# z1 of the last token chunk by seven block products, with the input weights scaled to fp16 in place

## The chip, the cores and the metric

The kernel runs on one core of one Trainium2 chip. The metric is the device time of one execution in microseconds (us); lower is better. The engines of the core are TensorE (PE, with its weight loads shown as PEld), VectorE (DVE), ScalarE (ACT), GpSimd (POOL) and SyncE (SP, which only issues DMAs here).

## The reference

One transformer-like block on 2048 tokens of 1024 channels, in bf16. First a local attention (8 keys at distance 2), then a gated MLP whose gate mixes over tokens:

```python
h  = x + A(layernorm(x))          # attention: qkv product, windowed softmax, output product
def B(x):                          # x = layernorm(h), 2048 x 1024
    z  = gelu(x @ w_in)            # w_in is 1024 x 3584
    z1 = z[:, :1792]
    z2 = layernorm(z[:, 1792:])
    g  = w_sp @ z2 + b_sp          # w_sp is 2048 x 2048: the spatial product
    return (z1 * g) @ w_out        # w_out is 1792 x 1024
out = h + B(layernorm(h))
```

## The kernel before

The 2048 tokens are worked in four chunks of 512 (CH). Up to the gate, all work is recorded as operations with a cost, a priority and dependencies in an object `Order`; its `run()` plans them with these costs on a model of the engines and the buffers and then emits them in the planned order, which is fixed from then on. Each engine works its instructions off in that order. What the plan says of times has no effect on the chip; waits come from the data and from reused memory.

The stages, in the order of time: q, k and v products; attention of the chunks 0 to 3 on DVE, under PE's products; `head(c)` (output product L719, residual `res` L725, layer norm, transposition of the normalized tokens into hnT by DMA on SP's queue); `b_z2(c)` (L796: z2 with the tokens as weights of the array, gelu and square on ACT, normalization on DVE, stores); `b_z1(c)` (L864: z1 transposed, features on the partitions; the input weights are the array's weights, 512 tokens the moving operand). Each chunk has seven pairs of 128-feature tiles; a pair fills one accumulator of two PSUM banks (`acc`, three of them), 16 matmuls of 512 columns, and ACT's gelu (L870) writes it out as z1s, whose row sums go to `zsum` and which a DMA stores in z1_d. The input weights of z1 lie in win2 (four pairs) and win3 (three pairs), bf16.

Then comes the spatial stage, written out by hand. It multiplies in blocks: a 2x2 partition of both factors is multiplied with seven products instead of eight (the Strassen and Winograd scheme), with sums and differences of blocks as operands, called forms. `load_raw` brings w_sp transposed into rawa and rawb, `scale_raw` (L958) scales it to fp16 by powers of two, `t_forms` (L965 to L971) makes three forms of it in the tiles form0 to form2 and one in place, `z_form` (L989) makes the forms of z2, which is read back from z2_d by `load_z2f`. `bias_rows` (L948) multiplies the scaled rows with the bias, from a tile `brow` in the pool bph. These are DVE operations of the planned part. Then the pools bph, ln1 and ps_acc are closed, and the pools p2 and psB open in the same memory. For each feature pair n, `row_one` multiplies the first block product into a bank `banka` (two of them) and ACT copies it to a tile p1 of p2; the products k4, k3 and k2 follow; `row_two` adds the second block product into the same `banka`:

```python
    def row_one(n, b11):
        firsts[n] = bank_a(), f32("p1", 3)
        times(firsts[n][0][:], slab(z2f[n][0][:, :, 0:P]), slab(b11), True)
        A.copy(firsts[n][1][:], firsts[n][0][:])

    def row_two(n, b21):
        times(firsts[n][0][:], slab(z2f[n][1][:, :, 0:P]), slab(b21), False)
```

DVE and POOL combine the products, multiply with z1 (read back by `load_z1c`, scaled by `z1_scaled` with the scales from `feature_scales`) and write zg, the operand of the output product, which is also done in blocks.

Of the kernel before, what the change touches and what calls it, by code (L numbers as in the profile page):

```python
# [10 lines left out]
FP32 = mybir.dt.float32  # L11
BF16 = mybir.dt.bfloat16
FP16 = mybir.dt.float16
# [9 lines left out]
P = 128  # L23
# [45 lines left out]
class Order:  # L69
# [6 lines left out]
    def add(self, eng, us, fn, deps=(), prio=5.0, lat=0.1, take=None, free=None, table=None):  # L76
        o = _Op()
        o.eng, o.us, o.fn, o.prio, o.lat, o.free, o.table = eng, us, fn, prio, lat, free, table
        o.take = (take,) if isinstance(take, str) else take or ()
        o.deps = [d if isinstance(d, tuple) else (d, d.lat) for d in deps if d is not None]  # L80
        o.start, o.end, o.n = None, None, len(self.ops)
        self.ops.append(o)
        return o
# [49 lines left out]
def kernel(  # L133
# [47 lines left out]
    rscT = cpool.tile([P, P], BF16, name="rscT")  # L181
    rinv = cpool.tile([P, NT], I32, name="rinv_w")
    zsum = mv1[:].rearrange("p a b -> p (a b)")[:, 0:NCH * (NF // 2)].rearrange("p (c f) -> p c f", c=NCH)
    babs = rstd1[:]

    w16 = ctx.enter_context(tc.tile_pool(name="w16", bufs=2))

# [9 lines left out]
    def new_acc():  # L197
        return ps_acc.tile([P, 2, CH], FP32, name="acc", tag="acc")
# [202 lines left out]
    def dma_op(us, fn, deps, lat=0.1, free=None):  # L401
        return add("DMA", us, fn, deps, lat=lat, free=free)
# [46 lines left out]
    def order():  # L449
        seq[0] += 1  # L450
        return 6.0 + seq[0] * 1e-3
# [402 lines left out]
    def b_z1(c):  # L854
        for fp in range(NF // 2):
            deps = [G["hnT", c], G["win", 2 if fp < 4 else 3]]
            for j, k0 in PIECES:
                def mm(j=j, k0=k0, fp=fp):
                    f = 2 * fp + j
                    wt, f0 = (wins[2], f) if f < 8 else (wins[3], f - 8)  # L860
                    if j == 0 and k0 == 0:
                        G["accy", c, fp] = new_acc()
                    for kt in range(k0, k0 + 4):
                        T.matmul(G["accy", c, fp][:, j, :].rearrange("p (a b) -> p a b", a=TPC), wt[:, kt, f0 * P:(f0 + 1) * P],  # L864
                                 hnTs[c][:, :, kt, :], start=(kt == 0), stop=(kt == KT - 1))
                m_ = add("PE", 0.8634, mm, deps, prio=order(), take="acc" if j == 0 and k0 == 0 else None)
                deps = [(m_, 0.0)]
            def ev(fp=fp):
                z1s = l1.tile([P, 2, CH], BF16, name="z1s", tag="xn", bufs=4)
                A.activation(z1s[:], G["accy", c, fp][:], ACTF.Gelu_apprx_tanh, accum_out=zsum[:, c, fp:fp + 1])  # L870
                last_store[:] = [(A.dma_start if c == NCH - 1 else dma)(z1_d[2 * fp:2 * fp + 2, :, c * CH:(c + 1) * CH].rearrange("f p s -> p f s"), z1s[:])]
            e_ = add("ACT", 0.93, ev, [m_], prio=2.0, free="acc", table="gelu", take="xn")
            dma_op(3.0, lambda: None, [e_], free="xn")
        G["z1done", c] = m_
        G["z1ev", c] = e_

    wsp_view = B_w_sp.rearrange("t (a p) -> t a p", p=P)
    raw, frm, wt_ = {}, {}, {}
# [2 lines left out]
    def wsp_sums():  # L881
        tl = {}
        for i in range(TPP):
            def ld(i=i):
                load_wn(i, l1, "x4k", 4)
            gate = add("DMA", WSP_FROM + WSP_EVERY * i, lambda: None)
            l_ = dma_op(8.0, ld, [gate, wabs_ops[i - 4] if i >= 4 else G["normed", 2]])
            if i >= WSP_HELD[0]:
                l_ = add("DMA", WSP_HELD[1], lambda: None)
            for hf in range(2):  # L890
                a_ = add("ACT", 1.22, lambda i=i, hf=hf: row_sum(i, hf), [l_], prio=5.8)
            wabs_ops.append(a_)
# [17 lines left out]
    def row_scales(pr):  # L910
        n = slice(pr * TPP, (pr + 1) * TPP)
        V.tensor_tensor(wlim[:, n], wabs[:, n, 0], wabs[:, n, 1], op=ALU.add)
        V.tensor_tensor(wlim[:, n], wlim[:, n], babs[:, n], op=ALU.add)
        V.tensor_scalar(wlim[:, n], wlim[:, n], 2.0 ** -40, 2.0 ** 60, op0=ALU.max, op1=ALU.min)
        V.tensor_scalar(wexp[:, n], wlim[:, n].bitcast(I32), 0x7F800000, None, op0=ALU.bitwise_and)
        V.tensor_scalar(rsc[:, n], wexp[:, n], -1.0, float(261 << 23), op0=ALU.mult, op1=ALU.add)
        V.tensor_scalar(rinv[:, n], wexp[:, n], float(-(7 << 23)), None, op0=ALU.add)
        V.tensor_copy(rsc16[:, n], rsc[:, n].bitcast(FP32))
# [33 lines left out]
            raw[c] = wtile([P, NT, CH], "rawa", "wB") if c % 2 == 0 else zpools["z"].tile([P, NT, CH], BF16, name="rawb")  # L952
        nc.sync.dma_start_transpose(raw[c][:, :, lo * P:hi * P], wsp_view[c * CH + lo * P:c * CH + hi * P])

    def scale_raw(c, k0):
        ks = slice(k0, k0 + HK)
        rows = wt_["rows"][:, c * CH:(c + 1) * CH].unsqueeze(1).to_broadcast([P, HK, CH])
        V.tensor_tensor(raw[c][:, ks, :].bitcast(FP16), raw[c][:, ks, :], rows, op=ALU.mult)  # L958

    def t_forms(pr, n):  # L960
        a, b = raw[2 * pr][:].bitcast(FP16), raw[2 * pr + 1][:].bitcast(FP16)
        if n < 3:
            frm[pr, n] = zpools["z"].tile([P, HK, CH], FP16, name=f"form{n}")
        if n == 0:
            V.tensor_tensor(frm[pr, 0][:], b[:, 0:HK, :], a[:, 0:HK, :], op=ALU.subtract)  # L965
        elif n == 1:
            V.tensor_tensor(frm[pr, 1][:], b[:, HK:NT, :], frm[pr, 0][:], op=ALU.subtract)
        elif n == 2:
            V.tensor_tensor(frm[pr, 2][:], a[:, HK:NT, :], frm[pr, 1][:], op=ALU.subtract)
        else:  # L970
            V.tensor_tensor(b[:, 0:HK, :], b[:, HK:NT, :], b[:, 0:HK, :], op=ALU.subtract)  # L971
# [42 lines left out]

    G["open"].deps.append((G["win", 1], 0.1))
    wsp_sums()
    for c in range(NCH):
        attention(c)
        if c == 2:
            G["win", 1].deps.append((G["kload", c], 0.1))  # L1020
        if c < NCH - 1:
            head(c)
# [15 lines left out]
        bias_in(0)  # L1038

    head(NCH - 1)  # L1040
    bt_ = add("PE", 0.1, bias_turned, [G["normed", 3]], prio=1.0, take="acc", lat=0.2)
    bs_ = add("ACT", 0.3, bias_size, [bt_], prio=2.0, free="acc")
    rs_ = add("DVE", 1.0, lambda: row_scales(0), [G["avdone", NCH - 1], bs_] + wabs_ops, prio=2.8)
    rt_ = add("PE", 0.1, rows_turned, [rs_], prio=0.5, take="acc", lat=0.2)
    ro_ = add("ACT", 0.3, rows_out, [rt_], prio=1.0, free="acc")
    rl_ = dma_op(4.0, rows_first, [(ro_, 2.5), G["close"]])
    b_z2(NCH - 1)
    b_z1(NCH - 1)
    r0_ = dma_op(4.0, lambda: load_raw(0, 0, 1), [G["close"], rl_.deps[0], (G["hnT", NCH - 1, 2], 0.0 - 3.9)])
    r0_ = dma_op(4.0, lambda: load_raw(0, 1, 2), [r0_, (G["hnT", NCH - 1, 3], 0.0 - 3.9)])  # L1050
    r0_ = dma_op(8.0, lambda: load_raw(0, 2, TPC), [r0_, (G["hnT", NCH - 1, 3], 0.0 - 3.9)])
    r1_ = dma_op(10.5, lambda: load_raw(1), [r0_])
    prev = []
    for c, r_ in ((0, r0_), (1, r1_)):
        for k0 in (0, HK):
            prev = [add("DVE", 2.3, lambda c=c, k0=k0: scale_raw(c, k0), [r_, rl_] + prev, prio=3.5)]
    z_ld = {}
    for n in range(2):
        for hf in range(2):
            z_ld[n, hf] = dma_op(6.0, lambda n=n, hf=hf: load_z2f(n, hf), [r1_] + [G["z2st", 2 * hf + c, il] for c in range(2) for il in range(TPC)])  # L1060
    for n in (0, 3):
        prev = [add("DVE", 2.3, lambda n=n: t_forms(0, n), prev, prio=3.6)]
    prev = [add("DVE", 0.7, lambda: z_form(0, 3), [z_ld[0, 0]] + prev, prio=3.6)]
    for n in (1, 2):
        prev = [add("DVE", 2.3, lambda n=n: t_forms(0, n), prev, prio=3.6)]
    for m in (1, 2, 4):
        prev = [add("DVE", 0.7, lambda m=m: z_form(0, m), [z_ld[0, 0], z_ld[0, 1]] + prev, prio=3.65)]
    add("DVE", 0.7, lambda: bias_rows(0), prev, prio=3.7)
    o_.run()
    wout_a = wtile([P, 8, D], "wout_a", "wA")  # L1070
# [36 lines left out]
    def row_two(n, b21):  # L1107
        times(firsts[n][0][:], slab(z2f[n][1][:, :, 0:P]), slab(b21), False)
# [18 lines left out]
    kb = p2.tile([P, 8], BF16, name="kb", tag="kb", bufs=1)  # L1127
    ones = p2.tile([1, P], BF16, name="ones", tag="ones", bufs=1)

    def pow2_of(out, x, sign, bias):  # L1130
        V.tensor_scalar(out.bitcast(I32), x.bitcast(I32), 0x7F800000, None, op0=ALU.bitwise_and)
        V.tensor_scalar(out.bitcast(I32), out.bitcast(I32), sign, float(bias << 23) if bias > 0 else -float(-bias << 23), op0=ALU.mult, op1=ALU.add)

    def feature_scales():
        V.tensor_reduce(zmax, zsum.rearrange("p c f -> p f c"), axis=AX.X, op=ALU.add)
        V.tensor_scalar(zmax, zmax, 800.0, 2.0 ** 60, op0=ALU.add, op1=ALU.min)
        pow2_of(sf, zmax, -1.0, 253)
        pow2_of(rf, zmax, 1.0, 1)

# [75 lines left out]
    for pr in range(NCH // 2):  # L1215
# [5 lines left out]
        for i in range(NQ):  # L1221
# [7 lines left out]
                zg = p2.tile([P, NF, 2 * CH], FP16, name="zg", tag="zg", bufs=1)  # L1229
            load_wout(n)  # L1230
            z1c = z1cs[n][:].bitcast(FP16)
            if n not in firsts:
                row_one(n, b11)
            k1, p1 = firsts[n]
# [14 lines left out]
            if pr == 0 and i == 5:  # L1249
# [4 lines left out]
                T.transpose(turned[0:1, P:2 * P], kb[:, 0:1], ident[:])  # L1254
                A.copy(rscT[0:TPP, :], turned[0:TPP, 0:P])
                A.dma_start(rs_d[TPP:NT, :], rscT[0:TPP, :])
            if n not in (NQ, NQ + 1):
                row_two(n, b21)
            times(k4[:], slab(a22), slab(t4_), False)
            nc.gpsimd.tensor_tensor(p7[:], p7[:], p5[:], op=ALU.add)  # L1260
# [207 lines left out]
```

## Time and profile before

| what | value |
|---|---|
| median of 3 runs | 690.81 us (690.63 to 690.89) |
| the profiled execution | 690.56 us, span 688.8 us |
| mean granted TensorE clock | 0.999 |
| PE busy | 683.4 us, 99% of the span |
| DVE busy | 563.1 us, 82% |
| ACT busy | 338.0 us, 49% |
| POOL busy | 148.1 us, 22% |
| z1, L864: 448 matmuls of 128x512 | 98.0 us of PE, a quarter of it for the last chunk |
| z2, L796: 512 matmuls | 98.0 us of PE |
| t_forms, L965 to L971, per pair of chunks | 4 operations of 2.28 to 2.29 us on DVE |

Times of the trace are counted from the span's start. The busy time of an engine is the time in which it works on an instruction; register, semaphore and DMA-issuing instructions are not in it. A matmul's own length in the trace (0.379 us for 512 columns) holds its way through the array; in a row, matmuls start closer than that.

### The profile page before, as it was taken

The page shows a single profiled execution, that of the slowest core. Times are in us where ns is not written, and L with a number is a line of the kernel's source. Part 1 is how long each engine was busy: PE and PEld are TensorE (multiplying, and loading weights), DVE is VectorE, ACT ScalarE, POOL GpSimd, SP SyncE. Part 2 cuts the span into 40 slices and gives each one's busy share as a digit, 9 for nine tenths or more (in the row PEclk, how much of TensorE's full clock was granted, in tenths as well). Part 3 has the DMA queues.
Part 4 walks back from the last instruction along what each step waited for, and adds up shares of the span by engine and source line. Part 5 has one row for each costly group of instructions (what it writes and reads, how often), then busy time and mean ns, then how long its engine had stood idle before and what let it go on. Part 6 is the DMA issues. An engine that isn't in the chain of part 4 may idle for free.

```text
span 688.8 us, 8981 instructions
## 1 busy us (share of the span) xinstructions
PE 683.4 (99%) x3374; PEld 354.2 (51%) x3374; DVE 563.1 (82%) x701; ACT 338.0 (49%) x487; POOL 148.1 (22%) x134
## 2 busy tenths in 40 slices
PE   9999999999999999999999999999999999999997
PEld 7766666566645445444544444444444444444443
DVE  6899899998999989998995358666789998665575
ACT  4547652354236886664882553387771122324121
POOL 0100010010110101100120131443441223553442
PEclk9999999999999999999999999999999999999999
DMA  9979588667995569453583999889968214552031
GB/s 326 325 242 246 176 194 268 154 164 265 227 349 212 111 246 237 154 175 98 130 217 128 209 239 323 273 242 289 250 186 215 89 62 118 157 152 94 0 119 65
DMA packets 145275, 133.05 MB, mean 193 GB/s; under 512 B 68752, under 2 KB 117296, under 8 KB 145104
## 3 DMA queue, kind: packets, MB, share of 16 engines
q1 hardware_dynamic: 132720, 88.93, 45.1%
q0 software_dynamic: 7856, 32.97, 17.0%
q10 hardware_dynamic: 4656, 10.59, 4.5%
q8 instruction: 26, 0.43, 0.3%
q14 instruction: 17, 0.14, 0.1%
HBM read 75.25 MB, written 33.10 MB: 157 GB/s over the span
## 4 chain that ended last, share of the span: by engine, by line
PE 98%; DMA 0%; DVE 0%; ACT 0%; issue 0%; DVEq 0%
PE bank L1092 25%; PE acc L464 22%; PE acc L796 14%; PE acc L864 14%; PE banka L1092 10%; PE acc L719 8%; PE acc L306 2%; PE bank L1343 1%; PE banka L1343 0%; DMA xp<-in_A_x_dram 0%; PE L L558 0%; PE pb L620 0%; PE tpt L302 0%; DVE bnst L261 0%; ACT xnT L303 0%; DVE hr L1428 0%
## 5 line engine op out<-in xcount | busy, mean ns | idle before, releaser
L864 PE MATMUL acc<-hnT,win 128*128 128x512 bf16 x448 | 98.0, 379 | 0.0
L796 PE MATMUL acc<-win,hnT 128*128 128x512 bf16 (+1 forms) x512 | 98.0, 352 | 0.0
L796 PEld LDWEIGHTS <-hnT 128*128 128x128 bf16 x512 | 49.9, 98 | 47.4 <-issue 0.7
L528 DVE TENSOR_TENSOR prod<-qT,kT 128x4096 bf16<-128x4096 bf16 x32 | 72.9, 2287 | 1.3 <-ACT kT L470 1.3
L1092 PEld LDWEIGHTS <-zs 128*128 128x128 f16 x448 | 43.7, 98 | 52.6
L864 PEld LDWEIGHTS <-win 128*128 128x128 bf16 x448 | 43.7, 98 | 52.6 <-issue 0.7
L475 ACT CAST stg<-acc 128x1024 bf16<-128x1024 f32 x36 | 36.4, 1012 | 60.7 <-PE acc L464 53.3
L464 PE MATMUL acc<-xnT,wk 128*128 128x512 bf16 x256 | 56.5, 379 | 0.0
L464 PE MATMUL acc<-xnT,wv 128*128 128x512 bf16 x256 | 56.4, 380 | 0.0
L719 PE MATMUL acc<-wo_sb,av_oT 128*128 128x512 bf16 x256 | 56.1, 379 | 0.0
L1092 PEld LDWEIGHTS <-z 128*128 128x128 bf16 x336 | 32.8, 98 | 39.5
L1092 PE MATMUL bank<-rawb,zs 128*128 128x512 f16 x224 | 52.8, 379 | 0.0
L1092 PE MATMUL banka<-rawa,z 128*128 128x512 f16 x224 | 52.4, 379 | 0.0
L1092 PE MATMUL bank<-form,zs 128*128 128x512 f16 x224 | 50.6, 379 | 0.0
L464 PEld LDWEIGHTS <-wk 128*128 128x128 bf16 x256 | 36.5, 143 | 19.1 <-issue 0.8
L464 PEld LDWEIGHTS <-wv 128*128 128x128 bf16 x256 | 36.5, 144 | 18.6 <-issue 0.5
L870 ACT ACTIVATE z1s<-acc 128x1024 bf16<-128x1024 f32 x28 | 28.6, 1022 | 34.6 <-PE acc L864 26.2
L803 ACT ACTIVATE u<-acc 128x1024 bf16<-128x1024 f32 (+1 forms) x32 | 29.3, 915 | 31.6 <-PE acc L796 31.6
L464 PE MATMUL acc<-xnT,wq 128*128 128x512 bf16 x192 | 41.9, 379 | 0.0
L719 PEld LDWEIGHTS <-av_oT 128*128 128x128 bf16 x256 | 24.9, 98 | 30.0
L532 DVE TENSOR_TENSOR prod<-prod 128x2048 bf16<-128x2048 bf16 x32 | 38.9, 1221 | 0.0
L464 PEld LDWEIGHTS <-wq 128*128 128x128 bf16 x192 | 27.5, 143 | 13.9
(271 smaller groups left out, 1112.5 us busy)
## 6 DMA issues: line engine op xcount, KB each, us to landing
z<-z_d SPq DMA_DIRECT2D x28, 512.0 KB, 5.0
qkv_d<-stg SPq DMA_DIRECT2D x36, 256.0 KB, 5.8
wn<-in_B_w_sp_dram ACTq DMA_DIRECT2D x16, 512.0 KB, 3.9
z1c<-z_d SPq DMA_DIRECT2D x14, 512.0 KB, 3.9
z_d<-z1s SPq DMA_DIRECT2D x21, 256.0 KB, 2.3
z_d<-u SPq DMA_DIRECT2D x12, 448.0 KB, 2.6
av_y<-av_z POOLq DMA_DIRECT2D x4, 1024.0 KB, 9.6
av_oT<-av_zz POOLq DMA_DIRECT2D x4, 1024.0 KB, 15.6
```

Of the source, the lines that this page charges most:

```text
L306: T.matmul(dst.rearrange("p (a b) -> p a b", b=P), wqs[:, kt, dl, :], xnT[0][:, lo:hi, kt, :], start=start, stop=stop)
L464: T.matmul(G[key][:, j, :].rearrange("p (a b) -> p a b", a=TPC), wv[:, kt, dl, :], xnT[c][:, :, kt, :], start=(kt == 0), stop=(kt == KT - 1))
L475: A.copy(stg[:], G[key][:])
L528: V.tensor_tensor(st["prod"][:], qT[:], kT[:, :, o:o + CH], op=ALU.mult)
L532: V.tensor_tensor(dst, p_[:, 0:4, :], p_[:, 4:8, :], op=ALU.add)
L719: T.matmul(st["acc", il][:, nh, :], oTs[c][:, dl, il * P:(il + 1) * P], wo_sb[:, dl, nh * CH:(nh + 1) * CH], start=(dl == 0), stop=(dl == ...
L796: T.matmul(accf[:, n0:n1], hnTs[c][:, il, kt, :], wins[hf][:, kt, n0:n1], start=(kt == 0), stop=(kt == KT - 1))
L803: A.activation(st["u", il][:, hf * 1024:hf * 1024 + wd], G["accz", c, il, hf][:].rearrange("p a b -> p (a b)")[:, 0:wd], ACTF.Gelu_apprx_t ...
L864: T.matmul(G["accy", c, fp][:, j, :].rearrange("p (a b) -> p a b", a=TPC), wt[:, kt, f0 * P:(f0 + 1) * P], hnTs[c][:, :, kt, :], start=(kt ...
L870: A.activation(z1s[:], G["accy", c, fp][:], ACTF.Gelu_apprx_tanh, accum_out=zsum[:, c, fp:fp + 1])
L1092: T.matmul(dst, wts(k), mov(k), start=(first and k == 0), stop=(k == last - 1), skip_group_check=not first)
L1343: T.matmul(acc[:], zg[:, f, (c1, c2)[t]:(c1, c2)[t] + P], wout_tile(f).bitcast(FP16)[:, nh * CH:(nh + 1) * CH], start=(f == 0), stop=(f == ...
```

## The change

The last chunk's z1 is computed by `b_z1_blocks` instead of `b_z1`. Weights (1024 channels by two feature tiles) and tokens (1024 channels by 512) are cut into 2x2 blocks (512 channels, 128 features, 256 tokens), and seven products replace eight. Each product of a pair is four matmuls of 256 columns. For this

- `w1_level` finds one power of two for the weights of win2 and win3: fourteen ACT sums of absolute values, a reduction on DVE, a one-column matmul with ones, an ACT copy, and two powers on DVE. `bias_turned` and `bias_size` are recorded earlier than before, since rscT is used for the ones.
- after the chunk before has used them, DVE scales win2 and win3 in place from bf16 to fp16 (four operations), and makes four forms of the weights for each (three in the tiles form0 to form2, one in place) and four forms of the tokens (hnf).
- the products are accumulated in four groups of feature pairs, (0, 1), (2, 3), (6) and (4, 5), in the order p1, p7, p5, p6, p2, p4, p3. ACT copies p1, p7 and p5 to a scratch tile, DVE and POOL form the sums (u, w, c21, c22, c12), partly in PSUM, and ACT's gelu takes the scale back and writes 256 tokens of each pair at a time. The second group uses the two `banka` banks beside the accumulators.
- `scale_raw` works in quarters; the z forms of the first pair stand between its t_forms, and each t_forms waits for the product of the last group that reads the tile it writes.
- `feature_scales` adds up the sums that now stand in two more columns (zmore).
- the first spatial pair opens with row_one(0), row_one(1), row_two(0), row_two(1).

The diff, cut to its core:

```diff
+    def b_z1_blocks(c, level):
...
+        for k in (2, 3):
+            for hk in range(2):
+                def sc(k=k, hk=hk):
+                    half = wins[k][:, 4 * hk:4 * hk + 4, :]
+                    V.tensor_scalar(half.bitcast(FP16), half, lev[:, 2:3], None, op0=ALU.mult)
+                scaled[k, hk] = add("DVE", 1.5 if k == 2 else 1.15, sc, [level, last_mm[k], G["avdone", c]], prio=2.7)
...
+        PRODS = (("k1", 1, 0), ("k4", 7, 0), ("k3", 5, 0), ("k2", 6, 0), ("k1", 2, 1), ("k4", 4, 1), ("k3", 3, 1))
+        groups = ((0, 1), (2, 3), (6,), (4, 5))
...
+                    for j, fp in enumerate(fps):
+                        t = fp if k == 2 else fp - 4
+                        for kt in range(4):
...
+                            T.matmul(d_, wt, mv, start=(not again and j == 0 and kt == 0 and not (g == 2 and b_)), stop=(j == len(fps) - 1 and kt == 3),
+                                     skip_group_check=bool(again) or g == 2)
...
+            u_ = dv("u", lambda pt=pt, Y=Y: V.tensor_tensor(pt(3), Y(1), pt(0), op=ALU.add), [ops[6], ops["cp", 1]] + ([before["c22"]] if before else []))
+            w_ = dv("w", lambda pt=pt: nc.gpsimd.tensor_tensor(pt(1), pt(1), pt(2), op=ALU.add), [ops["cp", 7], ops["cp", 5]], eng="POOL", us=1.26)
+            c21 = dv("c21", lambda pt=pt, X=X: V.tensor_tensor(X(1), X(1), pt(3), op=ALU.add), [ops[4], u_])
+            c22 = dv("c22", lambda pt=pt, Y=Y: V.tensor_tensor(Y(1), pt(1), pt(3), op=ALU.add), [u_, w_])
+            c12 = dv("c12", lambda pt=pt, Y=Y: V.tensor_tensor(Y(0), Y(0), pt(3), op=ALU.add), [ops[3], u_])
...
-    b_z1(NCH - 1)
+    z1ops = b_z1_blocks(NCH - 1, level1)
...
-        for k0 in (0, HK):
-            prev = [add("DVE", 2.3, lambda c=c, k0=k0: scale_raw(c, k0), [r_, rl_] + prev, prio=3.5)]
+        for k0 in range(0, NT, 4):
+            prev = [add("DVE", 1.2, lambda c=c, k0=k0: scale_raw(c, k0, 4), [r_, rl_] + prev, prio=3.5)]
...
-    for n in (0, 3):
-        prev = [add("DVE", 2.3, lambda n=n: t_forms(0, n), prev, prio=3.6)]
-    prev = [add("DVE", 0.7, lambda: z_form(0, 3), [z_ld[0, 0]] + prev, prio=3.6)]
-    for n in (1, 2):
-        prev = [add("DVE", 2.3, lambda n=n: t_forms(0, n), prev, prio=3.6)]
-    for m in (1, 2, 4):
-        prev = [add("DVE", 0.7, lambda m=m: z_form(0, m), [z_ld[0, 0], z_ld[0, 1]] + prev, prio=3.65)]
+    prev = [add("DVE", 0.7, lambda: z_form(0, 3), [z_ld[0, 0]] + prev, prio=3.55)]
+    for n, p_ in ((0, 5), (3, 5), (1, 6), (2, 3)):
+        prev = [add("DVE", 2.3, lambda n=n: t_forms(0, n), prev + [(z1ops[p_], 0.2)], prio=3.6)]
+        if n in (3, 1, 2):
+            m = {3: 1, 1: 2, 2: 4}[n]
+            prev = [add("DVE", 0.7, lambda m=m: z_form(0, m), [z_ld[0, 0], z_ld[0, 1]] + prev, prio=3.65)]
     add("DVE", 0.7, lambda: bias_rows(0), prev, prio=3.7)
...
+            if n == 0:
+                for m_ in (0, 1):
+                    row_one(m_, b11)
+                for m_ in (0, 1):
+                    row_two(m_, b21)
...
-            if n not in (NQ, NQ + 1):
+            if n not in (0, 1, NQ, NQ + 1):
                 row_two(n, b21)
```

## The prediction

> **What bounds the kernel now.** I read the page's busy shares and its chain first, then the timeline of TensorE (PE), VectorE (DVE) and ScalarE (ACT) around the change, then the busy time of four stretches.
>
> ```profile
> span 688.8 us, 8981 instructions
> ...
> PE 683.4 (99%) x3374; PEld 354.2 (51%) x3374; DVE 563.1 (82%) x701; ACT 338.0 (49%) x487; POOL 148.1 (22%) x134
> ...
> PE 98%; DMA 0%; DVE 0%; ACT 0%; issue 0%; DVEq 0%
> ```
>
> The first line of these is the span, the second the busy time of each engine, the third the chain that ended last. PE never waits: a matmul saved there is worth its full time, and any wait that the change puts in front of PE costs its full time, because nothing behind it has slack to give back.
>
> The timeline (start, length, engine, line, tiles, count) shows what PE does from the last token chunk's z1 (L864) on:
>
> ```profile
> 404.67 24.34 PE L864 MATMUL acc<-hnT,win 128*128 128x512 bf16 x112
> 428.85 1.89 PE L1092 MATMUL banka<-rawa,z 128*128 128x512 f16 x8
> 430.57 1.89 PE L1092 MATMUL bank<-rawb,zs 128*128 128x512 f16 x8
> 432.30 3.62 PE L1092 MATMUL bank<-form,zs 128*128 128x512 f16 x16
> 435.75 1.89 PE L1092 MATMUL banka<-rawa,z 128*128 128x512 f16 x8
> ```
>
> The spatial stage opens with row_one (428.85), and row_two, which adds into the same bank, comes only after 24 other matmuls (435.75). In that time ACT must copy row_one's product away. ACT and DVE there:
>
> ```profile
> 424.33 2.29 DVE L969 TENSOR_TENSOR form<-rawa,form 128x4096 f16<-128x4096 f16 x1
> 428.88 0.69 DVE L989 TENSOR_TENSOR zs<-z,z 128x1024 f16<-128x1024 bf16 x1 [2.27 <-DMA z<-z_d]
> ...
> 430.95 0.69 DVE L948 TENSOR_TENSOR rows<-rows,brow 128x1024 bf16<-128x1024 bf16 x1
> ...
> 430.19 0.37 ACTq L871 DMA_DIRECT2D z_d<-z1s  x1
> 432.50 0.59 ACT L1105 COPY p<-banka 128x512 f32<-128x512 f32 x1 [2.34 <-PE bank L1092]
> ```
>
> row_one ended at 430.74, but the copy started at 432.50. Its target p lies in the pool p2, which is laid over the released pools bph and ln1. In the built program the copy waits, among others, for bias_rows (L948), DVE's last reader of the old memory, and for the last z1 store. DVE was done at 431.64, after 2.27 us of idling; the store, issued at 430.19, lands some 2.3 us later by the page's DMA rows, at 432.5. In this kernel the wait is free, because PE did not need the copy until 435.75.
>
> DVE's room, by stretches (length, then busy time of PE, PEld, DVE, ACT, POOL):
>
> ```profile
> 380.50:404.70 24.20, 24.20 (x130) 12.50 (x129) 5.99 (x21) 14.68 (x24) 2.90 (x5) 1.00 1.01 212
> 404.70:428.90 24.20, 24.20 (x115) 11.00 (x113) 20.53 (x22) 9.38 (x16) 7.56 (x6) 1.00 1.08 308
> ```
>
> DVE is nearly free during z2 (18 us idle) and nearly full during z1 (3.7 us idle).
>
> **The change part by part.**
>
> Matmuls removed and added. 112 matmuls of 512 columns become 7 pairs x 7 products x 4 = 196 of 256 columns. L864 steps at (24.34 - 0.38)/111 = 0.216 us. The first projection shows 256 columns with a new weight each time:
>
> ```profile
> 15.19 8.03 PE L306 MATMUL acc<-xnT,wq 128*128 128x256 bf16 x72
> ```
>
> That is (8.03 - 0.27)/71 = 0.1093 us. So 24.18 becomes 21.42: **-2.8 us**. Mixed fp16 and bf16 operands already run at 0.216 in L1092 (z is bf16, rawa fp16).
>
> The weights' level. 14 ACT sums of 128x1024 (1.15 us each by L908, 16 us) fall in chunks 0 to 2, where ACT is half idle (49%); no PE operation waits for them but the one-column matmul that spreads the level. A tiny matmul among 512-column ones costs 0.25 us (L929: 366.49 to 366.64 plus 0.1 in front). **+0.25**. Bound: 0 to 1 us if one acc is freed late.
>
> Scaling the weights in place: four DVE operations, of 4096 and 3072 elements. L742 (1024 in 0.54) and L832 (1792 in 0.75) give 0.27 ns an element, so an estimate of 1.36 and 1.1 us; L1156, the same operation on z1c, took 0.75 to 1.60 for 2048, so up to 3.2. I take the low value (POOL is nearly idle there). They stand in head(3): two before the first residual, where DVE was idle 4.3 us, two between the later ones. The order on DVE also moves: the first tile's normalization now stands behind the second tile's variance, and its transpose on SP's queue behind the third h store. So it is issued after the third residual, at 376.35 + 1.31 + 0.3 = 377.9 instead of 374.65, and with 3.1 us to land comes at 381.0, where z2(3) was to start at 380.46. **+0.6**, bound 0 to 1.5.
>
> Forms of weights and tokens: 4 of 2048 elements at 1.22, 4 of 1536 at 0.95 (L1197), 4 of 1024 at 0.69: 11.4 us of DVE, in the 18 idle us of z2(3): **0**. Without that cover they would delay the first products one for one. The raw spatial rows are scaled in eight operations of 1.22 instead of four of 2.28, 0.6 us more on DVE in z1, which is counted below where it ends up, in the opening. Eight z1 stores instead of seven leave on ACT's queue, each issue 0.37 us of its sequencer and none of PE's time; feature_scales gets four operations of 0.17 on DVE after the opening: 0.
>
> Combining the products, per group of two pairs: ACT copies three (0.59), POOL adds two (1.26), DVE adds four (0.68 each, by L1295). This is inside z1, and PE's last products need it. First group: when products 5 and 6 are through, copy 0.59 + POOL 1.26 + DVE's c22 0.68 + some 0.35 of handing over = 2.9 must end before product 3; PE has two products, 16 x 0.109 = 1.75, to cover that: 1.15 wait. Second group: the copy of k4 stands on ACT behind the first group's 1.11-us gelu: 1.2. The single pair has products of 0.44 us against the same chain: 0.65 and 0.6. The last group reuses the one scratch p: 1.15. **+4.7**, bound 2.5 to 6.5.
>
> The opening. PE now does row_one(0), row_one(1), row_two(0), row_two(1). row_two(0) accumulates into the bank that ACT copies from, so it waits for that copy, and the copy waits for bias_rows. Between row_one(0) and row_two(0) PE has one row_one, 1.73 us, where it had 24 matmuls, 5.2 us. And bias_rows comes late: the T forms are written into form0 to form2, which z1's weight forms now hold, so t_forms(0) can't start before the last group's product 5 is through, and behind it in DVE's order stand, start to start: u 0.60, t_form 2.20, c21, c22, c12 1.93, then t_form 2.20, z_form 0.60, t_form 2.20, z_form 0.60, t_form 2.20, z_form 0.60, bias_rows 0.69 = 13.8 us. u starts 0.84 after product 6 (matmul's drain 0.16, copy 0.59, handing over). PE has from there three products, 2.62, and two row_ones, 3.46: 6.1 us. Idle: 0.84 + 13.8 + 0.7 (the copy) - 6.1 = **+9.3**, bound 8 to 11. What hid bias_rows, 24 matmuls and an early DVE, is gone.
>
> The clock after it. The kernel's first matmuls came from idle:
>
> ```profile
> 1.19 4.38 PE L228 MATMUL wps<-warm 128*128 128x512 bf16 x11 [1.19 <-DVE eps_t L231]
> ...
> 687.70:688.80 1.10, 0.00 (x0) 0.00 (x0) 0.00 (x0) 0.00 (x0) 0.00 (x0) 0.50 0.00 0
> ```
>
> Ten steps took 4.38 - 0.38 = 4.0 us instead of 2.16: 1.85 lost. The last line is a stretch at the end: 2.6 us after the last matmul (685.07) the granted clock is 0.50. So a PE idle for 9 us restarts at half clock: **+1.9**, bound 0 (the clock holds) to 3.7 (twice the start's loss). [...] The waits of about 1 us inside z1 are shorter than the 2.6.
>
> After the opening all of the first pair's forms are ready and DVE is level again; nothing is paid back, since PE had no later wait to lose.
>
> Sum: -2.8 + 0.25 + 0.6 + 4.7 + 9.3 + 1.9 = +13.95. The profiled execution took 690.56 (span 688.8 and 1.8 around it), so 704.5; the median of the runs is 0.25 above that execution: **704.8**.
>
> **The rivals.**
>
> The block products win. If DVE were through with bias_rows 4.6 us after it starts u (6.1 - 0.84 - 0.7), not 13.8, the opening would be free, and with the combining hidden too only -2.8 + 0.25 stay: 688.2. For it: z2(3)'s 18 idle us take the forms off z1, and the four products need none. Against: four T forms alone are 9.2 us by L965 to L971, and their memory is held until product 5. 0.04. Something between, with some 3 us of waits left, within 0.2%: 0.02.
>
> The copy waits for z1's stores alone. Counted from product 6: u and t_form 3.6, c21 0.6, two gelus 2.2, issue and landing 2.4, copy 0.7, less PE's 6.1: 3.5 us of wait instead of 9.3, with the clock's 1.9 about 698.9. For it: before, the copy followed the store's landing, not DVE. Against: the built program's wait on bias_rows. 0.09.
>
> DVE is slower still, its scalings at L1156's rate and its adds stretched beside POOL (L1313's mean is 0.84 where L1315's is 0.72): +3 to 4 us, of which head(3) hides part; with the clock's upper bound, 708. 0.07.
>
> 256-column matmuls are bound by weight loads (98 ns each): the 143-ns loads of L306 still gave 0.109, so 0.01; it would add some 10 us.
>
> **How the numbers follow.** The forecast has 0.77. The range reaches down to the store rival (698.9) and up to the slow DVE with the clock's upper bound: 698.5 to 709. A measurement here can tell about 0.2% (1.4 us) from no change. Faster 0.04, same 0.02, slower 0.94.
>
> **What would show it.** PE idle once for about 9 us between the 16th and 17th banka matmul of the opening, ended by ACT's copy, which follows bias_rows on DVE; 427-ns steps behind it; waits of about 1 us inside z1 ended by ACT or DVE; 196 matmuls stepping at 109 ns; a short wait ahead of z2(3) ended by hnT. I am wrong if PE goes straight from row_one into row_two, or if copy and bias_rows turn out not to be tied.

## The result and the profile after

The changed kernel takes 721.62 us (median of 4 runs, 717.57 to 724.37) where the kernel before, run beside it, takes 690.72: a ratio of 1.0443, 95% interval 1.0382 to 1.0504. It is slower by 30.9 us, more than twice the loss that was forecast (704.8 us), and outside the range (698.5 to 709). The profiled execution took 724.37 us, span 722.6.

The page of the profile after, the same three lines as before (span, busy time, chain of waits):

```profile
span 722.6 us, 9270 instructions
...
PE 686.6 (95%) x3459; PEld 363.3 (50%) x3459; DVE 586.8 (81%) x747; ACT 359.3 (50%) x532; POOL 156.2 (22%) x139
...
PE 93%; issue 3%; DVE 2%; ACT 1%; DMA 1%; POOL 0%; ACTq 0%; SPq 0%; DVEq 0%
```

PE, 99% busy before, is now at 95%, and new shares stand in the chain. The timeline of PE shows where (start, length, engine, line, operation, tiles, shape, count, and in brackets the idle time before it and who ended it):

```profile
381.20 24.39 PE L800 MATMUL acc<-win,hnT 128*128 128x512 bf16 x128 [0.70 <-DMA hnT<-hb]
...
409.79 1.04 PE L1019 MATMUL acc<-hnf,win 128*128 128x256 f16 x8
411.84 1.05 PE L1019 MATMUL acc<-hnT,form 128*128 128x256 bf16 x8 [1.01 <-DVE stot L823]
412.72 1.04 PE L1019 MATMUL acc<-hnT,win 128*128 128x256 bf16 x8
...
426.72 1.03 PE L1019 MATMUL acc<-hnf,win 128*128 128x256 f16 x8 [1.34 <-ACT hb L1035]
...
431.96 3.62 PE L1284 MATMUL banka<-rawa,z 128*128 128x512 f16 x16
445.37 6.41 PE L1284 MATMUL banka<-rawa,z 128*128 128x512 f16 x16 [9.79 <-ACT p L1297]
451.62 1.89 PE L1284 MATMUL bank<-rawb,zs 128*128 128x512 f16 x8
...
527.73 0.26 PE L1452 MATMUL bank<-ident,kb 128*1 128x128 bf16 x1 [15.37 <-issue]
527.93 3.59 PE L1284 MATMUL banka<-rawa,z 128*128 128x512 f16 x8
531.32 2.72 PE L1284 MATMUL bank<-form,z 128*128 128x512 f16 x8
```

All that was forecast is there: a short wait ahead of z2(3), waits of about 1 us inside z1 (five: 1.01, 1.08, 0.46, 0.43 and 1.34; for the first the profile names stot, but the sum c22, L1045, ended just ahead of it, at 411.78), matmuls of 256 columns 0.109 us apart (eight take 0.88, 412.72 - 411.84), and 9.79 us of idle between the 16th and 17th banka matmul. The last three lines are what no step of the prediction held: in spatial pair 5 PE stands for 15.37 us in front of the small transposition of kb (L1452). The releaser is given as "issue", so the chain has to be followed by hand, in the timelines of ACT and DVE:

```profile
444.74 1.07 ACT L1297 COPY p<-banka 128x512 f32<-128x512 f32 x2 [7.52 <-DVE rows L1140]
...
521.78 1.06 ACT L1337 ACTIVATE zg<-wout_b 128x1024 f16<-128x1024 bf16 x1 [18.60 <-DMA wout_b<-in_B_w_out_dram]
...
526.50 0.17 DVE L1353 TENSOR_TENSOR small<-small 128x7 f32<-128x7 f32 x1 [16.09 <-ACT zg L1337]
...
527.48 0.16 DVE L1358 CAST kb<-small 128x1 bf16<-128x1 f32 x1
```

The first of these lines is the opening: the copy waits for bias_rows, as forecast. The others are the late idle, backwards: kb is the last step of `wout_level` (L1353 to L1358), which waits for ACT's sums of the output weights (`wout_sum`, L1337), which wait for the load of their last megabyte, features 10 to 13. `load_wout` (L1342) issues it at pair 4 from POOL, on the software queue (q0 software_dynamic in the DMA view: 272 packets, 1.05 MB). On SP's queue, in the same pair, `load_raw` (L1145) issues the third piece of the transposing load of chunk 2. The timeline of before shows the two issues (start, and the time that issuing took):

```profile
477.32 0.91 POOL L1149 DMA_DIRECT2D wout_b<-in_B_w_out_dram  x1
...
479.53 7.03 SPq L953 DMA_TRANSPOSE rawa<-in_B_w_sp_dram  x1
```

Its DMA view gives the time from issue to landing in the last column:

```profile
wout_b<-in_B_w_out_dram POOLq DMA_DIRECT2D x1, 1024.0 KB, 8.0
rawa<-in_B_w_sp_dram SPq DMA_TRANSPOSE x1, 9.0
```

The same timeline of after:

```profile
495.39 6.38 SPq L1145 DMA_TRANSPOSE rawa<-in_B_w_sp_dram  x1
495.87 0.77 POOL L1342 DMA_DIRECT2D wout_b<-in_B_w_out_dram  x1
```

And its DMA view:

```profile
wout_b<-in_B_w_out_dram POOLq DMA_DIRECT2D x1, 1024.0 KB, 25.8
rawa<-in_B_w_sp_dram SPq DMA_TRANSPOSE x2, 25.8
```

Before, the load goes out 2.2 us ahead of the transposition and they take 8.0 and 9.0 us. After, it goes out 0.48 us behind, and both take 25.8. The windows view from the first issue of the two to the landing of both (length; busy time of PE, PEld, DVE, ACT, POOL; granted clock, DMA share, GB/s), before:

```profile
477.30:488.50 11.20, 11.20 (x54) 5.06 (x52) 7.66 (x12) 8.21 (x16) 4.83 (x5) 1.00 1.13 312
```

And after, with its first 4.6 us and 17 us from its midst:

```profile
495.40:500.00 4.60, 4.60 (x23) 2.10 (x22) 2.92 (x5) 2.32 (x6) 2.12 (x3) 1.00 1.09 314
500.00:517.00 17.00, 12.36 (x58) 5.40 (x56) 8.20 (x17) 3.19 (x7) 4.28 (x4) 0.97 1.23 85
495.40:521.70 26.30, 16.96 (x79) 7.49 (x77) 11.12 (x21) 5.51 (x11) 6.40 (x6) 0.89 1.16 154
```

At nearly the same DMA share (1.16 and 1.13) the core moves 154 GB/s instead of 312, and 85 in the midst, so the transfers do not merely share what there is. Below, a transfer that is slowed like this is said to crawl. What SP issues beside them crawls too: the median load of z takes 19.3 us where it took 6.2.

### The profile page after: what moved, and what is told of

The parts are those of the page before. It is cut to its first block, busy times and chain, and to the rows that moved or that the text cites. A ratio compares the mean times of both kernels' runs of the same rounds, so it can differ in the third digit from the quotient of the medians.

```text
span 722.6 us, 9270 instructions
## 1 busy us (share of the span) xinstructions
PE 686.6 (95%) x3459; PEld 363.3 (50%) x3459; DVE 586.8 (81%) x747; ACT 359.3 (50%) x532; POOL 156.2 (22%) x139
## 4 chain that ended last, share of the span: by engine, by line
PE 93%; issue 3%; DVE 2%; ACT 1%; DMA 1%; POOL 0%; ACTq 0%; SPq 0%; DVEq 0%
PE bank L1284 24%; PE acc L468 21%; PE acc L800 13%; PE acc L868 10%; PE banka L1284 10%; PE acc L723 7%; PE acc L1019 2%; PE acc L310 2%; PE bank L1541 1%; ACT hb L1035 0%; DMA hnT<-hb 0%; PE banka L1541 0%; DMA xp<-in_A_x_dram 0%; ACT z1s L1061 0%; DVE form L1159 0%
## 5 line engine op out<-in xcount | busy, mean ns | idle before, releaser
L868 PE MATMUL acc<-hnT,win 128*128 128x512 bf16 x336 | 73.7, 379 | 0.0
L1284 PE MATMUL banka<-rawa,z 128*128 128x512 f16 x224 | 56.6, 403 | 9.8 <-ACT p L1297 9.8
L868 PEld LDWEIGHTS <-win 128*128 128x128 bf16 x336 | 32.7, 98 | 39.5 <-issue 0.7
L1458 POOL TENSOR_TENSOR p<-p,p 128x512 f32<-128x512 f32 x14 | 21.1, 1508 | 71.9 <-ACT p L1445 48.8
L1297 ACT COPY p<-banka 128x512 f32<-128x512 f32 x14 | 8.0, 582 | 53.9 <-PE banka L1284 46.4
```

Source lines behind the costliest of these rows:

```text
L1284: T.matmul(dst, wts(k), mov(k), start=(first and k == 0), stop=(k == last - 1), skip_group_check=not first)
```

## The experiments

Theory A: the load crawls because it starts together with the transposing load, and the new opening is what brought the two together. Rival B: ACT and DVE are behind PE after the opening, and their chain to kb is late by itself. Line numbers are those of the changed kernel, in a fence those of the kernel that ran. "Off" in the table below is the issue of the load less that of pair 4's transposing load.

**e1: the same load at pair 1.**

```diff
-    WLOAD = {0: ((0, 4), (4, 6)), 1: ((6, 8), (8, 10)), 4: ((10, 14),)}
+    WLOAD = {0: ((0, 4), (4, 6)), 1: ((6, 8), (8, 10), (10, 14))}
```

> The changed kernel, with the last megabyte of the output weights (wout_b, features 10 to 13) loaded at spatial pair 1 instead of pair 4. Theory A (the load runs together with the transposing load of the third raw chunk, both crawl from 8 to 26 us, and ACT's sums, VectorE's level and PE's transposition of it wait): the idle of 15.5 us at the transposition in pair 5 and its 2.3 us of half clock are gone, 703 to 707 us. Rival B (the chain of ACT and VectorE to that transposition is late because the opening left both behind PE): the idle stays, 717 to 724 us.

Measured: 707.66 us (707.20 to 708.47), ratio 1.0248 [1.0232, 1.0263]. The load takes 9.8 us; the idle at kb is 0.97 us in place of 15.37, with another 0.82 ahead of the small product behind it (L1499). The time is 0.7 us over what A gave. B falls: with the opening untouched, moving one DMA takes back 14 us.

**e2: the kernel before, with the load behind GpSimd's first addition of pair 4.**

```diff
-            load_wout(n)
+            if n != 4:
+                load_wout(n)
...
             nc.gpsimd.tensor_tensor(p7[:], p7[:], p5[:], op=ALU.add)
+            if n == 4:
+                load_wout(n)
```

> The kernel before, with the same load issued later within pair 4: on GpSimd's queue behind its first addition of the pair, so about 2 to 4 us behind the transposing load on SP's queue, where it was 2.2 us ahead. Theory A (issued behind the transposition, the load crawls): before gets an idle of 10 to 18 us at the transposition in pair 5, 703 to 710 us. Rival B (the load needs 8 us wherever it is issued, and only the opening's lag makes it late): 690.7 us, within 0.5.

Measured: 693.27 us, ratio 1.0039 [1.0024, 1.0054]. It went out 4.9 us behind and took 7.0 us. So "behind" in itself does nothing, and A in that form is wrong. The time lies in neither range. What it cost are two short waits of PE in pair 5 (0.96 and 1.22), since the load lands 7 us later than in the kernel before.

**e3: the changed kernel with the opening of before**, so the block products alone.

```diff
-            if n == 0:
-                for m_ in (0, 1):
-                    row_one(m_, b11)
-                for m_ in (0, 1):
-                    row_two(m_, b21)
...
-            if n not in (0, 1, NQ, NQ + 1):
+            if n not in (NQ, NQ + 1):
```

> The changed kernel with the four products of the opening back in the order of before (row_one, three products, row_two). Theory A: PE waits some 3.4 us for the first pair's form 3 and some 2.4 us for the copy, 5.8 in place of 10.0, without a half clock or with up to 2 us of it; PE is then less far ahead of GpSimd, the load goes out ahead of the transposition, no late idle: 699 to 703 us. Rival (block products alone put GpSimd behind): 715 to 720 us with the late idle.

Measured: 700.51 us, ratio 1.0145 [1.0130, 1.0160]. The load is 2.2 us ahead again and takes 8.7; no idle at kb. The timeline of PE has one wait in the opening:

```profile
438.70 3.59 PE L1284 MATMUL bank<-rawb,zs 128*128 128x512 f16 x8 [3.97 <-DVE rawb L1163]
442.09 4.92 PE L1284 MATMUL bank<-form,zs 128*128 128x512 f16 x16
```

The half clock behind the 3.97 us (granted clock 0.50 from 438.7 to 444.0) stretches the products that follow: 8 matmuls take 3.59 us instead of 1.89, and 16 take 4.92 instead of 3.62. So PE comes to row_two only at 446.85, when ACT's copy (445.61, 0.59 us long) is done, and the copy adds no idle.

**e4: the kernel before with the new opening alone.**

```diff
+            if n == 0:
+                for m_ in (0, 1):
+                    row_one(m_, b11)
+                for m_ in (0, 1):
+                    row_two(m_, b21)
...
-            if n not in (NQ, NQ + 1):
+            if n not in (0, 1, NQ, NQ + 1):
```

> The kernel before with only the opening changed (row_one of pairs 0 and 1, then row_two of both). Theory A: row_two waits for the copy, 0.8 us, VectorE was done with its forms before and has no lag, so the load keeps its place ahead of the transposition: 691 to 692.5 us. Rival B (the opening by itself makes the lag): an idle at the transposition in pair 5, 700 us or more.

Measured: 691.76 us, ratio 1.0019 [1.0010, 1.0029]; 0.67 us of idle for the copy, and 0.92 and 1.23 in pair 5 in the profiled execution, the slowest of the ten (693.72). The load is no longer 2.2 us ahead of the transposition; it goes out 0.05 us ahead and takes 11.9 us. The opening makes that shift by itself, and the expectation's "no lag" was wrong. The two parts alone cost 1.1 and 9.8 us; together they cost 30.9. About 14 of these come with the load's crawl; without it (e1, e10) the two together cost 17, since the opening then waits 9.79 us and not 3.97 as in e3.

**e5: bias_rows ahead of the T forms.**

```diff
+    prev = [add("DVE", 0.7, lambda: bias_rows(0), prev, prio=3.5)]
     z_ld = {}
...
-    add("DVE", 0.7, lambda: bias_rows(0), prev, prio=3.7)
```

> The changed kernel with the bias rows' product (bias_rows) put on VectorE ahead of the T forms; the scheduler then also takes the last group's three combining additions ahead of the first T form. If the opening's 10 us are VectorE's queue in front of bias_rows, as forecast, row_two then waits for the copy behind z1's last store only: 3 to 4 us of idle in place of 10. The half clock may stay (2 us). What the late idle in pair 5 does is open: GpSimd is no earlier while PE is 6 us earlier, so the load of the output weights goes out 4 to 7 us behind the transposing load. If the crawl needs the two to start within about a microsecond: 698 to 703 us. If it comes whenever the load is behind: 713 to 717 us. If the copy waits for something else of VectorE: the opening stays at 9 us or more.

Measured: 717.72 us (709.65 to 719.03), ratio 1.0359 [1.0294, 1.0424]. The copy now waits for z1's last store, as the rival of the prediction had it, but that store takes longer than its 2.4 us. ACT's timeline has the issue of the store and the copy that waits for its landing:

```profile
437.04 0.37 ACTq L1062 DMA_DIRECT2D z_d<-z1s  x1
441.73 1.07 ACT L1297 COPY p<-banka 128x512 f32<-128x512 f32 x2 [4.71 <-DMA z_d<-z1s]
```

So the opening's idle falls from 9.79 to 6.31 and not to 3 to 4, and the time lies in no range of the expectation. The load comes 0.46 us behind the transposition, not 4 to 7 (GpSimd came earlier along with PE), takes 22.3 us, and the idle at kb is 11.8.

**e6: e5's edit and e1's together.**

> The bias rows early as in the run beside it, and the last megabyte of the output weights at pair 1: opening 3 to 4 us of idle, no idle over 2 us in pair 5. 707.7 less 6 to 7: 700 to 702 us.

Measured: 704.90 us, ratio 1.0212 [1.0196, 1.0227], for the same reason above what was expected: 5.83 us of idle in the opening.

**e7: the load ahead of GpSimd's last additions of pair 3.**

```diff
-            load_wout(n)
+            if n != 4:
+                load_wout(n)
...
+            if n == 3:
+                load_wout(4)
             nc.gpsimd.tensor_tensor(p1[:], u[:], bt1, op=ALU.add)
```

> The changed kernel, with the load of pair 4's output weights issued on GpSimd's queue ahead of its last additions of pair 3, so 3 to 4 us earlier and some 3 us ahead of the transposing load instead of 0.5 behind. Theory A (both crawl only when the transposition goes first by little): the load takes 8 to 10 us, the idle of 15.5 us is gone, 705 to 709 us. Rival (any overlap of the two after the new opening crawls, or the chain is late by itself): 717 to 724 us.

Measured: 708.82 us, ratio 1.0264 [1.0249, 1.0279]. The load went out 6.3 us ahead of pair 4's transposing load (3 had been aimed at; it is 5.8 behind pair 3's) and took 6.4 us; 1.02 us of idle at kb.

**e8: the transposing loads in pairs 2, 3, 5, 6.**

```diff
-            if pr == 0 and 2 <= i < 2 + TPC:
-                load_raw(2, i - 2, i - 1)
+            if pr == 0 and i in (2, 3, 5, 6):
+                q_ = (2, 3, 5, 6).index(i)
+                load_raw(2, q_, q_ + 1)
```

> The changed kernel with the load of the output weights where it is, and the transposing loads of the third raw chunk issued in pairs 2, 3, 5 and 6 instead of 2, 3, 4 and 5, so that none stands within 8 us of that load. Theory A (it is these two together): the load lands in 6 to 9 us, no idle over 2 us in pair 5, 705 to 709 us. Rival (the load crawls beside any other traffic after the new opening): 716 to 724 us.

Measured: 710.18 us, ratio 1.0281 [1.0266, 1.0297]. The load at its place takes 9.5 us with no transposition beside it, and no idle at kb is left. It is 1 us over what was expected, with 1.88 us of idle at L1499 and 2.44 us ahead of the output stage's block products; no other version waits there. So the late idle needs these two loads together, and it goes whichever of them is moved.

**e9 and e11: the kernel before, with two additions, and with one, that nobody waits for**, on GpSimd at the end of pair 3 (e11 has `range(1)`).

```diff
             nc.gpsimd.tensor_tensor(z22, p7[:], u[:], op=ALU.add)
+            if n == 3:
+                for _ in range(2):
+                    nc.gpsimd.tensor_tensor(p5[:], p7[:], u[:], op=ALU.add)
```

> The kernel before, with two more additions into a scratch tile on GpSimd at the end of pair 3 (2.5 us that nobody waits for), so that the load of the output weights is issued some 0.3 us behind the transposing load as in the changed kernel, where it was 2.2 us ahead. Theory A: the two loads crawl to some 25 us and an idle of 10 to 16 us comes at the transposition in pair 5, 702 to 709 us. Rival (the crawl needs something else of the changed kernel, or is chance): 691 to 694 us.

> The kernel before with one more addition on GpSimd at the end of pair 3 (1.2 us): the load of the output weights goes out some 1 us or less ahead of the transposing load, where it was 2.2 ahead, and 1.2 behind with two additions. If the transposition must be first for the crawl: 690.3 to 691.5 us. If starting within about a microsecond is enough, whoever is first: single runs up to 695 to 700 us.

Measured, two additions: median 693.02 us, ratio 1.0045 [1.0015, 1.0075], but single runs from 690.85 to 701.15. The median is the rival's, the slowest runs are not. In the profiled execution (697.54) the load is 1.18 us behind, where 0.3 had been aimed at, takes 15.0 us, and PE's timeline has the idle of the changed kernel:

```profile
501.95 0.26 PE L1254 MATMUL bank<-ident,kb 128*1 128x128 bf16 x1 [5.24 <-issue]
```

One addition: 690.81 us (690.52 to 691.89), ratio 1.0002 [0.9992, 1.0011]; 0.5 us ahead, 10.6 us to land. So the two additions bring the same effect with nothing of the change in the kernel, smaller, and from run to run very different.

**e10 and e14: the changed kernel with the load later**, by e2's edit and by one addition of e11's kind.

> The changed kernel with the load of the output weights issued later within pair 4, behind GpSimd's first addition of the pair: some 5 us behind the transposing load instead of 0.5. Theory A (they crawl when they start within about a microsecond of each other): the load takes 7 to 9 us and lands at about 508, ACT's four sums (4.7 us) and the level are done at about 514 where PE is at 512: an idle of 1 to 3 us, 706 to 710 us although the load starts later than in the changed kernel. Rival (any load behind the transposition crawls): 720 to 728 us.

> The changed kernel with one more addition into a scratch tile on GpSimd at the end of pair 3, so that the load goes out on the software queue some 1.5 to 2 us behind the transposing load instead of 0.5: the partner of the run beside it. If the software queue crawls near the start of a transposition: 15 us or more to land, as in the kernel before with two additions (1.2 us behind), 713 to 724 us. If the crawl is gone at that distance, as it was at 4.9 us: 706 to 709 us.

Measured: e10 707.43 us, ratio 1.0249 [1.0232, 1.0266], 4.9 us behind, 6.3 us to land. e14 707.57 us, ratio 1.0243 [1.0227, 1.0259], 1.75 us behind, 10.2 us to land. A load that starts later lands 15 to 16 us earlier. In e10's timeline, the issue and the sum that waits for it:

```profile
499.34 0.77 POOL L1342 DMA_DIRECT2D wout_b<-in_B_w_out_dram  x1
...
505.71 1.06 ACT L1337 ACTIVATE zg<-wout_b 128x1024 f16<-128x1024 bf16 x1 [3.50 <-DMA wout_b<-in_B_w_out_dram]
```

**e12 and e13: the load from ScalarE's hardware queue**, placed behind its copy of row_one's product, and behind its copy of k4's.

```diff
-            load_wout(n)
+            if n != 4:
+                load_wout(n)
...
+            if n == 4:
+                A.dma_start(wout_b[:, 2:6, :], wout_view[:, 10:14, :])
```

> The changed kernel with pair 4's load of the output weights issued on ScalarE's hardware queue, right behind its copy of row_one's product, instead of on GpSimd's software queue: at about 495.6 us, within half a microsecond of the transposing load as in the changed kernel. If the crawl belongs to the software queue beside a transposition: the load takes 7 to 11 us, the long idle in pair 5 is gone, 705 to 709 us. If any megabyte started at that moment crawls: 25 us to land and 715 to 724 us.

> As the run before on ScalarE's hardware queue, but with the load issued behind ScalarE's copy of k4's product, about 1 to 1.5 us behind the transposing load. If the crawl belongs to the software queue: 7 to 12 us to land, 705 to 710 us. If it belongs to the order, whatever the queue: 15 to 26 us to land, 713 to 724 us.

Measured: e12 707.08 us, ratio 1.0233 [1.0216, 1.0250], but it went out 0.4 us ahead of the transposition and so told nothing of the side behind; 10.9 us. e13 713.06 us, ratio 1.0326 [1.0307, 1.0344], 1.4 us behind, 13.5 us to land, 4.0 us of idle at kb. The time is that of the second expectation, at its lower end; 13.5 us lies between the two. The hardware queue is slowed as well, so the crawl is not the software queue's alone.

The profiled executions in order of the offset:

| off (us) | run | load (us) | transposing load (us) |
|---|---|---|---|
| -6.3 | e7 | 6.4 | 9.0 |
| -2.2 | before / e3 | 8.0 / 8.7 | 9.0 / 9.7 |
| -0.5 | e11 | 10.6 | 11.7 |
| -0.4 | e12, hardware queue | 10.9 | 12.2 |
| -0.05 | e4 | 11.9 | 13.4 |
| +0.46 | e5 | 22.3 | 22.5 |
| +0.48 | after | 25.8 | 25.8 |
| +1.18 | e9 | 15.0 | 15.9 |
| +1.4 | e13, hardware queue | 13.5 | 14.7 |
| +1.75 | e14 | 10.2 | 11.8 |
| +4.9 | e2 / e10 | 7.0 / 6.3 | 6.3 / 9.4 |

e1 and e6 issue the load some 7 us ahead of pair 2's transposing load, and e8 issues none in pair 4; they are not in the table. Among these executions the price is highest where the load starts half a microsecond behind the transposition, and most of it is gone 2 us to either side: 8.0 us to land at -2.2, 10.2 at +1.75, and 6.3 to 7.0 only at +4.9. Each figure is of one execution, and runs of one kernel differ (e5: 709.65 to 719.03), so the table gives no exact curve.

## Why the prediction was wrong

The forecast terms, against the trace after:

- Matmuls: -2.8 forecast, and 0.109 us a step measured.
- The weights' level: +0.25 forecast; nothing of it shows. PE starts the last matmuls of chunk 2's z1 at 379.47, before at 379.60.
- z2(3) waits for hnT: +0.6 forecast, 0.70 measured.
- Waits inside z1: +4.7 forecast in five waits of 0.6 to 1.2; five measured, 4.3 of idle, and 5.1 from start to start (the first, for instance, 411.84 against 409.79 + 8 x 0.109).
- Opening: +9.3 forecast, 9.79 measured. DVE's u starts at 430.17, 0.83 after product 6, as forecast, and bias_rows ends 14.4 us later (13.8): the first T form took 2.86 us.
- Half clock behind it: +1.9 forecast, 16 banka matmuls in 6.41 instead of 3.62, so 2.8. The rows of before had no stall inside the kernel to show; now there are several, of 3.97 (e3), 9.79 and 15.37 us among others, each with 427-ns steps and a granted clock of 0.50 behind it. The 1.9 was the author's estimate from the first matmuls of before, and its bound of 3.7 covers the 2.8. In the windows view of after, the granted clock falls at 440.8, 5.2 us after PE stopped, and is back at 1.00 from 451.1, 5.7 us after PE started again; in pair 5 it falls at 515.9, 3.5 us after PE stopped, and is back from 533.0, 5.3 us after PE started again.

These make -2.8 + 0.7 + 5.1 + 9.8 + 2.8 = 15.6 on 690.7: 706.3. The four versions of the changed kernel in which the load alone is moved, e1, e7, e10 and e14, stand at 707.4 to 708.8, with another 1.5 to 2.3 us of short waits in pair 5, inside the range. The rest of the loss is the late idle, 15.4 us, and the half clock behind it (granted clock 0.50 from 528 to 532): 3.59 and 2.72 instead of 1.89 each, 2.5 us. 706.3 + 17.9 = 724.2, and the profiled execution took 724.37.

The step that failed is "DVE is level again; nothing is paid back, since PE had no later wait to lose". DVE is level when the opening ends: the first pair's last form (443.29, 0.69 us long) is done before row_two starts at 445.37. It doesn't stay so. The opening takes four products ahead, so pairs 0 and 1 last 40 matmuls each on PE (8.6 us instead of 12.1), while DVE's additions `u` follow each other in 10.5 to 10.7 us (459.43, 469.89, 480.40, 491.08). Nor could DVE work ahead: of the second pair's forms it made one (444.50) and then idled 8.36 us, until PE had used the first pair's. Here are u in pair 3, GpSimd's addition that waits for it, and row_one(4), from the timelines of the three engines, before:

```profile
472.89 0.68 DVE L1295 TENSOR_TENSOR u<-bank,p 128x512 f32<-128x512 f32 x1
473.65 1.15 POOL L1296 TENSOR_TENSOR p<-u,rows 128x512 f32<-128x512 f32 x1 [1.23 <-DVE u L1295]
477.19 1.89 PE L1092 MATMUL banka<-rawa,z 128*128 128x512 f16 x8
```

And after:

```profile
491.08 0.68 DVE L1493 TENSOR_TENSOR u<-bank,p 128x512 f32<-128x512 f32 x1
491.85 1.16 POOL L1494 TENSOR_TENSOR p<-u,rows 128x512 f32<-128x512 f32 x1 [3.43 <-DVE u L1493]
493.06 1.89 PE L1284 MATMUL banka<-rawa,z 128*128 128x512 f16 x8
```

u was 4.3 us ahead of row_one(4) and is now 2.0 ahead. GpSimd has as many additions as before; it waits 3.43 us for u. Its load stands in its queue behind the additions, so it goes out 2.81 us behind row_one(4) instead of 0.13. SP's transposing load follows PE: it goes out 2.3 behind row_one(4) in both traces (before 477.19 to 479.53, after 493.06 to 495.39). So the margin of 2.2 us between the two issues is gone, and the crawl brings the later wait that the step denied. The step was argued from PE's row of before, in which there is no wait, and said nothing of the margins behind that row; DVE, GpSimd and SP were not followed through the pairs behind the opening. Even so, the profile before held no row with the price: what it showed of these two was 8.0 and 9.0 us side by side.

The opening alone shifts the load from 2.2 to 0.05 us ahead (e4, u 2.5 ahead of row_one(4)), the block products alone leave it at 2.2 (e3, u 4.3 ahead), and both together bring it 0.48 behind. That the load's crawl carries the late idle is shown from both sides, by moving either load (e1, e7, e8, e10, e14) and by setting the offset in the kernel before (e9). Why two transfers slow each other so much at just this offset is not settled. The rival "DVE slower still" was not it (the opening's idle came within 0.5 us of the forecast), and "256-column matmuls are bound by weight loads" did not come (0.109 us a step).

The best version of the change here is e3, 700.5, and nothing points to one that beats the kernel before: the waits inside z1 alone (5.1) cost more than the products save (2.8).

## What to carry to other kernels

A kernel with no waits is not a kernel without margins: for each order that is changed, list the DMA issues of every queue behind it with the engine that each one follows, and see which of them change places. Where the parts of a change were priced alone, run them together before adding the prices up (1.1 and 9.8 made 30.9). And when a wait shows only "issue", follow it by hand from tile to tile until a DMA or an engine's queue is reached.

## What the runs showed of the hardware

- A 1-MB load and a transposing load that had started half a microsecond ahead of it took 25.8 us each, in place of 8.0 and 9.0 with the load 2.2 us ahead. While they were in flight the core moved 154 GB/s instead of 312, at a DMA share of 1.16 and 1.13: the transfers in flight do not merely divide the rate of before between them, in all they moved less.
- The length of the crawl differs from run to run with one and the same kernel. Where the load on GpSimd's queue starts 0.4 to 1.2 us behind the transposition in the profiled execution, single runs lie far apart (e9: 690.85 to 701.15; the changed kernel: 717.57 to 724.37; e5: 709.65 to 719.03). The kernel before stayed between 690.23 and 691.20 in all that ran.
- In the changed kernel, waits of PE of up to 1.34 us inside z1 left the granted clock at 1.00 (406 to 431). How long PE had stood when the clock fell to 0.50 was not one length: 5.2 us in the opening, 3.5 in pair 5, and 2.5 at the end of the kernel before (687.6, the last matmul done at 685.07). Nor did the price follow the idle's length: 3.0 us were lost behind an idle of 3.97 (e3: 1.7 on the first 8 matmuls, 1.3 on the next 16), 2.9 behind 6.31 (e5: 16 matmuls in 6.54 instead of 3.62), 2.8 behind 9.79 and 2.5 behind 15.37.
